# Loading phi a second time with tokens on partitions, in place of turning it on TensorE

## The chip, the cores and the metric

The kernel runs on one NeuronCore of a Trainium2 chip. The metric is the device time of one execution in microseconds (us). The kernel before took 540.55 us (median of three runs, 540.34 to 540.92). Five engines work side by side and meet only at semaphores: PE (TensorE: matmuls and transposes through an identity matrix), DVE (VectorE), ACT (ScalarE), POOL (GpSimd) and SP (SyncE, which here only issues DMAs). Each works off its own instructions strictly in order.

## The reference

For each of 8 batches and 8 heads, 576 tokens attend to 32 "memories"; the result goes through a bilinear feed-forward network.

```python
a = phi - np.max(phi, axis=2, keepdims=True)        # phi (b, h, s, m): the max is over the tokens s
a = np.exp(a)
a = a / (np.sum(a, axis=2, keepdims=True) + 1e-09)  # and so is the sum
k_m = np.einsum('bhsm,bhsd->bhmd', a, k)            # contraction over the tokens
v_m = np.einsum('bhsm,bhsd->bhmd', a, v)
scores = scale * np.matmul(q, k_m.transpose(0, 1, 3, 2))
attn = softmax(scores) over m;  attn_out = attn @ v_m
x = attn_out as (tokens, 512);  out = ((x @ w1) * (x @ w2)) @ w3 @ w_out
```

The two ways in which `phi` is used pull apart: maximum and sum run over the tokens, so they want the tokens along the free dimension; the contraction `a^T k` runs over the tokens as well, and a matmul contracts over the partitions, so it wants the tokens there.

## The kernel before, in words

Weights are converted and multiplied together once, at the start (a long order written out by hand, `START`). Then a loop runs over the 8 batches. In iteration b PE does for batch b the two large products: 16 units "A" (`ab_unit`, L528: 12 matmuls each, 6 into a PSUM bank `a` and 6 into a bank `b`), and then the output products "O" (`out_part`, L558). Between them it does the attention of batch b+1 and the first attention steps of batch b+2. The order of PE's and SP's instructions is the order of the lists `FIRST`, `SECOND` and `STEADY` (L44 to L54), word by word; a "+" after a word means batch b+2, and `phi3`, `kv3`, `q2` are the loads of batches b+3 and b+2. In the loop DVE's and ACT's orders are not written by hand: a scheduler chooses them.

One unit "A" works like this: PE fills `a` (6 matmuls) and `b` (6 matmuls); ACT copies `a` to SBUF (`a_sb`, L550); DVE multiplies `b` by `a_sb` to `gr` (L553); ACT rounds `gr` to `gh` (L130); DVE computes the rest `gl = gr - gh` (L132). The banks `a` and `b` exist twice each, so PE may write bank `b` of unit n+2 only when `gr` of unit n is done, and bank `a` of unit n+2 when `a_sb` of unit n is done.

The first attention steps of a batch, in iteration b for batch b+2: `phi` is loaded with (head, memory) on the 128 partitions and the 576 tokens along the free dimension, in two halves t of four heads each (tile `ph`, 128x1152, DMA at L143). Then

- `top` (L183): DVE takes the negated maxima, one per partition and half: `mx`, 128x2.
- `exp` (L189): two ACT instructions, exp(ph + mx) in place, and the sums `sm` on the way.
- `norm` (L198): two small DVE instructions turn `sm` into its reciprocal.
- `turn0`, `turn4` (L203): PE transposes 8 and 1 blocks of 128x128 of `ph` into PSUM, ACT copies them to the tile `a` (128x1024 at L213 and 128x128 at L218): now the tokens are on partitions.
- `mem` (L220): 80 small matmuls of `a` with `kv`, after the 16 units A; ACT scales the result by `sm`.

The tile `a` shares its place in SBUF with `s_sb`, the scores of the batch whose attention is being computed after `mem`.

SP issues all loads and stores. In an iteration of the steady kind the last store of the output products (L585) is issued just after PE has begun the next iteration's first unit A, since ACT must copy the result out of PSUM first (L584). The next DMAs in SP's order are the `kv` loads (L154), which wait until `mem` has freed the place of the previous `kv`.

The iterations that turn a batch of number 3 or more: iteration 1 turns batch 2 (as the word `turn0`) and batch 3 (as `turn0+`); iterations 2 to 5 turn batches 4 to 7.

Of the kernel before, what the change touches and what calls it, by code (L numbers as in the profile page):

```python
# [8 lines left out]
F32 = mybir.dt.float32  # L9
# [4 lines left out]
AF = mybir.ActivationFunctionType  # L14
ALU = mybir.AluOpType
# [29 lines left out]
O O blocks O sc0 sc1p Mp se0 q2 sn0 O O kv2 pr0 O O O se1 sn1 O Mp Mp M O pr1 O phi2 O O O O O  # L45
""".split()
SECOND = """
A top exp A norm turn0 A turn4 A phi2 mem A kv2 blocks A A A A top+ A exp+ A norm+ A turn0+ A A turn4+ A A
mem+ sc0 sc1p Mp O kv3 se0 O se1 O q2 sn0 O pr0 O sn1 O pr1 M Mp Mp O O phi3 O O blocks+ O O O O O O Oo Oo Oo Oo
""".split()  # L50
STEADY = """
A top+ A exp+ A norm+ A A turn0+ A A turn4+ A A A A A A A A A
mem+ sc0 sc1p Mp O kv3 se0 O se1 O q2 sn0 O pr0 O sn1 O pr1 M Mp Mp O O phi3 O O blocks+ O O O O O O Oo Oo Oo Oo
""".split()  # L54


# [1 line left out]
def memory_attention__then__bilinear_ffn_kernel(  # L58
# [2 lines left out]
    qT: bass.AP,  # L61
    kv: bass.AP,
    phiT: bass.AP,
    weights: bass.AP,
    out: bass.AP,
):
# [10 lines left out]
    nc = tc.nc  # L77
    P = 128
    B, NG, S = qT.shape[0], 4, 576
    D = 64  # L80
    M = 32
    NT = 2
    DF = 1024
    weights = weights.bitcast(I32)
# [5 lines left out]

    const = ctx.enter_context(tc.tile_pool(name="const", bufs=1))
    att = ctx.enter_context(tc.tile_pool(name="att", bufs=1))
    ps_ab = ctx.enter_context(tc.tile_pool(name="ps_ab", bufs=2, space=bass.MemoryType.PSUM))
    ps_o = ctx.enter_context(tc.tile_pool(name="ps_o", bufs=2, space=bass.MemoryType.PSUM))
    ps_x = ctx.enter_context(tc.tile_pool(name="ps_x", bufs=1, space=bass.MemoryType.PSUM))
# [15 lines left out]
    for x, where in (("h", Wh), ("l", Wl)):  # L111
        t = const.tile([P, half, DO], F32R, name=f"W{x}0")
# [21 lines left out]
    def whole(step):  # L134
        for _ in step:
            pass


    loaded = {}
# [25 lines left out]
        loaded["q", b] = t  # L165
        yield

    LOADS = {"phi": load_phi, "kv": load_kv, "q": load_q}

    def load(what, b):  # L170
        b += int(what[-1])
        if b < B:
            return LOADS[what[:-1]](b)
        return ()
# [4 lines left out]
    def attention(b):  # L179

        v = {}

        def top():  # L183
            v["ph"] = loaded.pop(("ph", b))
            v["mx"] = att.tile([P, NT], F32, name="mx")
            nc.vector.tensor_reduce(out=v["mx"], in_=v["ph"], axis=AX.X, op=ALU.max, negate=True)
            yield

        def exp():  # L189
            v["sm"] = att.tile([P, NT], F32, name="sm")  # L190
            ph, mx, sm = v["ph"], v["mx"], v["sm"]
            for t in range(NT):
                nc.scalar.activation(
                    out=ph[:, t], in_=ph[:, t], func=AF.Exp, bias=mx[:, t : t + 1], accum_out=sm[:, t : t + 1]
                )
                yield

        def norm():  # L198
            nc.vector.tensor_scalar_add(v["sm"], v["sm"], 1e-9)
            nc.vector.reciprocal(out=v["sm"], in_=v["sm"])  # L200
            yield

        def turn(i):  # L203
            ps = psum_pair().rearrange("p k (c t x) -> p (k c) t x", c=2, t=NT)
            if i == 0:
                for c in range(4):
                    for t in range(NT):
                        at = t * D + c * P
                        nc.tensor.transpose(ps[:, c, t], v["ph"][:, t, at : at + P], ident)  # L209
                yield  # L210
                a = att.tile([P, 5 * NT * P], F32, name="a", tag="a")
                v["a"] = a.rearrange("p (c t x) -> p c t x", t=NT, x=P)
                nc.scalar.copy(out=v["a"][:, :4], in_=ps)  # L213
            else:
                last = v["ph"].rearrange("p t s -> p (t s)")[:, 4 * P : 5 * P]
                nc.tensor.transpose(ps[:, 0, 0], last, ident)
                yield
                nc.scalar.copy(out=v["a"][:, 4, 0], in_=ps[:, 0, 0])  # L218
# [84 lines left out]
        def probs(n):  # L303
# [7 lines left out]
            yield  # L311
            yield from split(ah[:, n], al[:, n], v["at"][:, n])

        steps = {"top": top, "exp": exp, "norm": norm, "mem": memories, "blocks": blocks}
        steps |= {f"turn{i}": lambda i=i: turn(i) for i in (0, 4)}
        for n in range(2):
            steps |= {f"sc{n}": lambda n=n: scores(n, pair), f"sc{n}p": lambda n=n: scores(n, banks_ab)}
# [7 lines left out]
    def memory_weights(b):  # L325

        ms = ready["M", b] = []

        def step(q, banks):
            one = None if banks else psum_pair()  # L330
            ps = banks() if banks else [one[:, t] for t in range(NT)]
            for g in range(NG):
                for t in range(NT):
                    d = slice((1 - t) * D, (2 - t) * D)
                    nc.tensor.matmul(  # L335
                        ps[t][g * M : (g + 1) * M],
                        lhsT=vm[b % 2][d, g],
                        rhs=w12_sb[q][d, :, g],
                        start=True,
                        stop=True,  # L340
                    )
            yield
            mh = const.tile([P, NT, 2, FQ], F32R, name=f"mh{q}", tag=f"m{m_tags[2 * q]}")
            ml = const.tile([P, NT, 2, FQ], F32R, name=f"ml{q}", tag=f"m{m_tags[2 * q + 1]}")
            if banks:
                for t in range(NT):
                    yield from split(mh[:, t], ml[:, t], ps[t].rearrange("p (w f) -> p w f", w=2))
            else:
                yield from split(mh, ml, one.rearrange("p t (w f) -> p t w f", w=2))
            ms.append((mh, ml))  # L350
            yield

        return [lambda banks=None, q=q: step(q, banks) for q in range(NQ)]
# [125 lines left out]
    def by_hand():  # L479
        return tc.manual_schedule(engines=set(HAND) | {mybir.EngineType.Activation, mybir.EngineType.DVE})  # L480

    steps = [attention(b) for b in range(B)]
    m0 = memory_weights(0)
    a0 = [(n, 2 * q + f) for q in range(NQ) for n in range(2) for f in range(2)]
    under_way = {}

    def begin(what):
        name, digits = what.rstrip("0123456789."), what.lstrip("abcdefghijklmnopqrstuvwxyzACGHKLNW")
        if name in LOADS:
            return load(what, 0)  # L490
# [67 lines left out]
    def out_part(b, i, part, v):  # L558

        first = 0 if b % 2 else REST  # L560
        at = first + i * P
        if part == 0:
            v["p"] = psum(ps_o, "o")
        for f in range(part * NF // 4, (part + 1) * NF // 4):
            for k, (x, y) in enumerate(((gh, Wh), (gl, Wh), (gh, Wl))):
                nc.tensor.matmul(  # L566
                    v["p"],
                    lhsT=x[f][:, at : at + P],
                    rhs=y[f],
                    start=f == 0 and k == 0,  # L570
                    stop=f == NF - 1 and k == 2,
                )
        if part < 3:
            return
        osb = big.tile([P, DO], F32, name="osb", bufs=2)
        if at == 0:
            nc.scalar.copy(out=osb, in_=v["p"])
            for j in range(2):
                c = (b - 1 + j) * S
                nc.sync.dma_start(out=out[c : c + REST], in_=osb[j * REST : (j + 1) * REST])  # L580
            return
        c = b * S + at - b % 2 * REST
        if b + 1 < B or at + P < S:
            nc.scalar.copy(out=osb, in_=v["p"])  # L584
            nc.sync.dma_start(out=out[c : c + P], in_=osb)  # L585
        else:
            for j, copy in enumerate((nc.scalar.copy, nc.vector.tensor_copy)):
                x = slice(j * DO // 2, (j + 1) * DO // 2)
                copy(out=osb[:, x], in_=v["p"][:, x])
                nc.sync.dma_start(out=out[c : c + P, x], in_=osb[:, x])  # L590
# [5 lines left out]
    for b in range(B):  # L596
        v = {}
# [5 lines left out]
        def emit(what):  # L603
# [4 lines left out]
            elif what == "Oo":  # L608
                if b % 2:
                    out_part(b, *next(parts), v)  # L610
            elif what[:-1] in LOADS:
                whole(load(what, b))
# [11 lines left out]
            emit(what)  # L624


_INS = ["qT", "kv", "phiT", "weights"]
_OUT = (4608, 512)


# [52 lines left out]
```

## Time and profile before

| | |
|---|---|
| Time, median of three runs | 540.55 us (540.34 to 540.92) |
| The profiled execution: its time, its span | 540.96 us, 539.0 us |
| Busy: PE, DVE, ACT | 525.2 us (97%), 310.1 us (58%), 252.8 us (47%) |
| Granted TensorE clock | 1.0 (full) |
| DMA queues of the program | 30.8% of 16 engines' span |
| Instructions | 9799 |

The span runs from the first instruction to the last; 1.96 us of the execution lie around it. PE's matmuls overlap, so one matmul's duration is longer than the time by which it moves the next one on; the chain of work that ended last gives each group of PE's matmuls the time that it really took up.

### The profile page before, as it was taken

Reading aid. Unit: us, or ns where it says so; the run is one execution under the profiler, and the core shown is the slowest. Engines: PE = TensorE matmul, PEld = TensorE weight load, DVE = VectorE, ACT = ScalarE, POOL = GpSimd, SP = SyncE. Lnnn points to the kernel's source line nnn. Section 1 sums busy time; section 2 is a strip of 40 time slices with the busy share of each in tenths; the row PEclk is TensorE's granted clock in tenths of the full one; section 3 lists DMA queues with packets and bytes.
Section 4 is the critical chain, followed back from the end, with each engine's and each line's share of the span. In section 5 each row is a group of like instructions: output and inputs, shape, how many; then the busy total and the mean of one; then the engine's idle time right before and its main releaser. Section 6 shows DMA issues by size and latency. Waiting matters only on the chain.

```text
span 539.0 us, 9799 instructions
## 1 busy us (share of the span) xinstructions
PE 525.2 (97%) x4056; PEld 432.8 (80%) x4056; DVE 310.1 (58%) x594; ACT 252.8 (47%) x510; POOL 0.7 (0%) x6
## 2 busy tenths in 40 slices
PE   4999989999999999999999999999999999999997
PEld 1457678868996799868986899769986898689985
DVE  5889999493658425683569235763577056905400
ACT  6998886353654325443544244344544144414310
POOL 0000000000000000000000000000000000000000
PEclk9999999999999999999999999999999999999999
DMA  8999616082607210342015200631021100010011
GB/s 335 420 419 420 272 45 264 2 294 93 221 1 283 84 39 2 123 183 82 1 63 223 102 20 1 223 125 40 2 89 40 39 21 2 21 58 2 1 39 60
DMA packets 14940, 64.07 MB, mean 119 GB/s; under 512 B 1712, under 2 KB 1968, under 8 KB 10032
## 3 DMA queue, kind: packets, MB, share of 16 engines
q1 hardware_dynamic: 14896, 63.45, 30.8%
q8 instruction: 32, 0.52, 0.4%
q14 instruction: 12, 0.10, 0.1%
HBM read 54.00 MB, written 9.44 MB: 118 GB/s over the span
## 4 chain that ended last, share of the span: by engine, by line
PE 92%; DVE 5%; DMA 1%; ACT 1%; issue 1%; DVEq 0%; ACTq 0%
PE o L566 37%; PE a L540 18%; PE b L540 18%; PE a L463 3%; PE b L463 3%; PE a L335 2%; PE o L228 2%; PE x L335 2%; DVE w L417 1%; PE x L209 1%; PE b L335 1%; PE x L228 1%; DMA ph<-in_phiT 1%; PE o L463 1%; PE x L270 1%
## 5 line engine op out<-in xcount | busy, mean ns | idle before, releaser
L553 DVE TENSOR_TENSOR gr<-b,a_sb 128x288 f32<-128x288 f32 x128 | 58.2, 457 | 85.4 <-PE b L540 83.1
L130 ACT CAST gh<-gr 128x288 fp32r<-128x288 f32 x128 | 55.3, 435 | 97.6 <-DVE gr L553 97.4
L566 PE MATMUL o<-W,gh 128*128 128x512 f32 x288 | 96.7, 396 | 0.0
L132 DVE TENSOR_TENSOR gl<-gr,gh 128x288 fp32r<-128x288 f32 x128 | 58.4, 458 | 57.2 <-ACT gh L130 56.9
L540 PE MATMUL b<-ah,mh 128*128 128x288 f32 x256 | 75.5, 295 | 1.7 <-DVE gr L553 1.7
L540 PE MATMUL a<-ah,mh 128*128 128x288 f32 x256 | 77.0, 301 | 0.1
L540 PE MATMUL b<-al,mh 128*128 128x288 f32 x256 | 75.5, 295 | 0.0
L540 PE MATMUL a<-ah,ml 128*128 128x288 f32 x256 | 75.5, 295 | 0.0
L540 PE MATMUL a<-al,mh 128*128 128x288 f32 x256 | 75.5, 295 | 0.0
L540 PE MATMUL b<-ah,ml 128*128 128x288 f32 x256 | 75.4, 294 | 0.0
L566 PEld LDWEIGHTS o<-W,gh 128*128 128x128 f32 x288 | 54.1, 188 | 17.3 <-issue 5.9
L584 ACT COPY osb<-o 128x512 f32<-128x512 f32 x31 | 18.1, 585 | 100.3 <-PE o L566 88.2
L566 PE MATMUL o<-Wh,gh 128*128 128x512 f32 x144 | 57.1, 397 | 0.0
L566 PE MATMUL o<-Wh,gl 128*128 128x512 f32 x144 | 56.4, 392 | 0.0
L566 PE MATMUL o<-Wl,gh 128*128 128x512 f32 x144 | 56.4, 392 | 0.0
L566 PE MATMUL o<-W,gl 128*128 128x512 f32 x144 | 56.4, 391 | 0.0
L550 ACT COPY a_sb<-a 128x288 f32<-128x288 f32 x128 | 50.4, 396 | 3.7 <-PE a L540 3.4
L540 PEld LDWEIGHTS a<-ah,mh 128*128 128x128 f32 x256 | 48.1, 188 | 3.3 <-issue 1.0
L540 PEld LDWEIGHTS b<-ah,mh 128*128 128x128 f32 x256 | 48.1, 188 | 2.4 <-DVE gr L553 2.2
L540 PEld LDWEIGHTS a<-al,mh 128*128 128x128 f32 x256 | 48.2, 188 | 0.3
L540 PEld LDWEIGHTS b<-ah,ml 128*128 128x128 f32 x256 | 48.1, 188 | 0.0
L540 PEld LDWEIGHTS a<-ah,ml 128*128 128x128 f32 x256 | 48.1, 188 | 0.0
(134 smaller groups left out, 770.3 us busy)
## 6 DMA issues: line engine op xcount, KB each, us to landing
kv<-in_kv SPq DMA_DIRECT2D x16, 1024.0 KB, 7.1
raw<-in_weights SPq DMA_DIRECT2D x10, 1024.0 KB, 18.0
q<-in_qT SPq DMA_DIRECT2D x8, 1152.0 KB, 10.0
out<-osb SPq DMA_DIRECT2D x31, 256.0 KB, 2.0
raw<-in_weights SPq DMA_DIRECT2D x12, 512.0 KB, 9.1
ph<-in_phiT SPq DMA_DIRECT2D x8, 576.0 KB, 4.1
kv<-in_weights SPq DMA_DIRECT2D x3, 1024.0 KB, 16.6
kv<-in_kv SPq DMA_DIRECT2D x8, 256.0 KB, 8.4
```

What stands on the lines that cost most here:

```text
L130: nc.scalar.copy(out=hi, in_=src)
L132: nc.vector.tensor_tensor(out=lo, in0=src, in1=hi.bitcast(F32), op=ALU.subtract)
L209: nc.tensor.transpose(ps[:, c, t], v["ph"][:, t, at : at + P], ident)
L228: nc.tensor.matmul(ps[t][h * M : (h + 1) * M, : 2 * D], lhsT=v["a"][:, i, t, h * M : (h + 1) * M], rhs=kvt[i][:, (4 * t + h) * 2 * D : (4 ...
L270: nc.tensor.matmul(ps[t][g * M : (g + 1) * M], lhsT=km[b % 2][t * D : (t + 1) * D, g], rhs=v["q"][t * D : (t + 1) * D, g, n * HALF : (n + ...
L335: nc.tensor.matmul(ps[t][g * M : (g + 1) * M], lhsT=vm[b % 2][d, g], rhs=w12_sb[q][d, :, g], start=True, stop=True,)
L463: nc.tensor.matmul(pw[r][i], lhsT=x[:, i * P : (i + 1) * P], rhs=y, start=k == 0 and j == 0, stop=k == NF - 1 and j == len(pairs) - 1,)
L540: nc.tensor.matmul(p, lhsT=x[:, t, w, fc : fc + P], rhs=y[:, n, t * HALF : (t + 1) * HALF], start=i == 0, stop=i == len(todo) - 1,)
L550: nc.scalar.copy(out=a_sb, in_=ps[0])
L553: nc.vector.tensor_tensor(out=gr, in0=ps[1], in1=a_sb, op=ALU.mult)
L566: nc.tensor.matmul(v["p"], lhsT=x[f][:, at : at + P], rhs=y[f], start=f == 0 and k == 0, stop=f == NF - 1 and k == 2,)
L584: nc.scalar.copy(out=osb, in_=v["p"])
```

## The change

From batch 3 on PE no longer turns `phi`. Instead `phi` is loaded a second time (`load_rows`), laid out by the host with the tokens on partitions, straight into the tile `a`. There the maxima are needed as a row along the free dimension, the same on all partitions. So:

- `row`: DVE's 32x32 block transpose turns the 128x2 maxima, padded to 128x32 (`mx32`, which POOL once sets to zero), into `turned`; four DMAs of 2x32 elements write them to a small tensor in HBM; one DMA reads it back as a row of 256 elements for each of the 128 partitions (`all`).
- `less`: one DVE instruction of 128x1024 and two of 64x128 add the (negated) maxima to `a`; one ACT instruction takes exp of 128x1152 in place.

`top`, `exp` and `norm` stay as they were: the sums `sm` still come from the first copy. The word `row+` stands in the lists behind `top+`, `less+` before the last five units A, `rows3` (the second load, of batch b+3) behind `phi3`. Batches 0 to 2 are turned on PE as before.

```diff
 SECOND = """
-A top exp A norm turn0 A turn4 A phi2 mem A kv2 blocks A A A A top+ A exp+ A norm+ A turn0+ A A turn4+ A A
-mem+ sc0 sc1p Mp O kv3 se0 O se1 O q2 sn0 O pr0 O sn1 O pr1 M Mp Mp O O phi3 O O blocks+ O O O O O O Oo Oo Oo Oo
+A top exp A norm turn0 A turn4 A phi2 mem rows2 A kv2 blocks A A A A top+ row+ A exp+ A norm+ A A A less+ A A
+mem+ sc0 sc1p Mp O kv3 se0 O se1 O q2 sn0 O pr0 O sn1 O pr1 M Mp Mp O O phi3 rows3 O O blocks+ O O O O O O Oo Oo Oo Oo
 """.split()
 STEADY = """
-A top+ A exp+ A norm+ A A turn0+ A A turn4+ A A A A A A A A A
-mem+ sc0 sc1p Mp O kv3 se0 O se1 O q2 sn0 O pr0 O sn1 O pr1 M Mp Mp O O phi3 O O blocks+ O O O O O O Oo Oo Oo Oo
+A top+ row+ A exp+ A norm+ A A A A A A A A less+ A A A A A
+mem+ sc0 sc1p Mp O kv3 se0 O se1 O q2 sn0 O pr0 O sn1 O pr1 M Mp Mp O O phi3 rows3 O O blocks+ O O O O O O Oo Oo Oo Oo
 """.split()
...
+    def load_rows(b):
+        t = att.tile([P, 5 * NT * P], F32, name="a", tag="a")
+        loaded["rows", b] = t
+        nc.sync.dma_start(out=t[:, : 9 * P], in_=phi[b])
+        yield
...
         def top():
             v["ph"] = loaded.pop(("ph", b))
-            v["mx"] = att.tile([P, NT], F32, name="mx")
+            v["mx"] = mx32[:, :NT] if b >= BY_ROWS else att.tile([P, NT], F32, name="mx")
             nc.vector.tensor_reduce(out=v["mx"], in_=v["ph"], axis=AX.X, op=ALU.max, negate=True)
...
+        def row():
+            turned = att.tile([P, M], F32, name="turned")
+            nc.vector.transpose(out=turned, in_=mx32)
+            mx = dram.tile([NT, NG, M], F32, name="mx")
+            for g in range(NG):
+                nc.sync.dma_start(out=mx[:, g], in_=turned[g * M : g * M + NT])
+            v["all"] = att.tile([P, NT * P], F32, name="all")
+            nc.sync.dma_start(out=v["all"], in_=mx.rearrange("t g m -> (t g m)").partition_broadcast(P))
+            yield
+
+        def less():
+            a = loaded.pop(("rows", b))
+            v["a"] = a.rearrange("p (c t x) -> p c t x", t=NT, x=P)
+            x = a[:, : 8 * P].rearrange("p (c x) -> p c x", c=4)
+            mx = v["all"].rearrange("p (c x) -> p c x", c=1)
+            nc.vector.tensor_tensor(out=x, in0=x, in1=mx.broadcast_to([P, 4, NT * P]), op=ALU.add)
+            for t in range(NT):
+                x = a[t * D : (t + 1) * D, 8 * P : 9 * P]
+                nc.vector.tensor_tensor(out=x, in0=x, in1=v["all"][t * D : (t + 1) * D, t * P : (t + 1) * P], op=ALU.add)
+            yield
+            a = a[:, : 9 * P]
+            nc.scalar.activation(out=a, in_=a, func=AF.Exp)
+            yield
...
+    BY_ROWS = 3
+    mx32 = const.tile([P, M], F32, name="mx32")
+    nc.gpsimd.memset(mx32, 0.0)
     steps = [attention(b) for b in range(B)]
```

Where the words of `less` land in DVE's and ACT's orders is the scheduler's choice. In the program `less+` stands behind the eleventh unit A of a steady iteration. DVE's order in iteration 3 around the first units A (each `gr` and each `gl` is one unit's) was before:

```order
L186 TENSOR_REDUCE mx<-ph 128x2
L199 TENSOR_SCALAR sm<-sm 128x2
L200 RECIPROCAL sm<-sm 128x2
L553 TENSOR_TENSOR gr<-b,a_sb 128x288
L132 TENSOR_TENSOR gl_624<-gr,gh_616 128x288
L553 TENSOR_TENSOR gr<-b,a_sb 128x288
L132 TENSOR_TENSOR gl_624<-gr,gh_616 128x288
L553 TENSOR_TENSOR gr<-b,a_sb 128x288
L132 TENSOR_TENSOR gl_625<-gr,gh_617 128x288
L553 TENSOR_TENSOR gr<-b,a_sb 128x288
```

and the same place now:

```order
L194 TENSOR_REDUCE mx_92<-ph 128x2
L208 STREAM_TRANSPOSE turned<-mx_92 128x32
L231 TENSOR_SCALAR sm<-sm 128x2
L232 RECIPROCAL sm<-sm 128x2
L588 TENSOR_TENSOR gr<-b,a_sb 128x288
L134 TENSOR_TENSOR gl_628<-gr,gh_620 128x288
L588 TENSOR_TENSOR gr<-b,a_sb 128x288
L134 TENSOR_TENSOR gl_628<-gr,gh_620 128x288
L588 TENSOR_TENSOR gr<-b,a_sb 128x288
L221 TENSOR_TENSOR a<-a,all 128x1024
L224 TENSOR_TENSOR a<-a,all 64x128 x2
L134 TENSOR_TENSOR gl_629<-gr,gh_621 128x288
```

The three instructions of `less` (L221, L224) stand behind the third unit's `gr`, ahead of its `gl` and of the fourth unit's `gr`; iterations 2, 4 and 5 have the same order. For batch 3, in iteration 1, they stand behind the eleventh unit's `gr`.

ACT's order in iteration 3, from the third unit's copy on (`gh` are the casts of `gr`), is now:

```order
L585 COPY a_sb<-a 128x288
L132 CAST gh_621<-gr 128x288
L585 COPY a_sb<-a 128x288 x2
L227 ACTIVATE a<-a 128x1152
L132 CAST gh_621<-gr 128x288
L132 CAST gh_622<-gr 128x288
L585 COPY a_sb<-a 128x288 x2
```

The new exp (L227) stands behind the fifth unit's copy and ahead of the fourth unit's cast; the copies of PSUM to `a` (L213, L218) are gone from it.

SP's order at the border of iterations 2 and 3, from the load of `phi` in iteration 2 to the `kv` loads of iteration 3, was before:

```order
L143 DMA ph<-in_phiT 128x1152
L585 DMA out<-osb 128x512 x2
L154 DMA kv_3113<-in_kv 128x2048
L154 DMA kv_3115<-in_kv 128x2048
L159 DMA kv_3117<-in_kv 128x512
```

and is now:

```order
L145 DMA ph<-in_phiT 128x1152
L173 DMA a<-in_phi 128x1152
L620 DMA out<-osb 128x512 x2
L211 DMA mx<-turned 2x32 x4
L213 DMA all<-mx 128x256
L156 DMA kv_3117<-in_kv 128x2048
```

The four small writes and the read stand behind the last store of an iteration; the read waits for all four writes, the writes for DVE's transpose.

More of the change, by code (lines that the diff above doesn't have):

```diff
@@ L63, in memory_attention__then__bilinear_ffn_kernel @@
     phiT: bass.AP,
+    phi: bass.AP,
     weights: bass.AP,
@@ L92, in memory_attention__then__bilinear_ffn_kernel @@
     att = ctx.enter_context(tc.tile_pool(name="att", bufs=1))
+    dram = ctx.enter_context(tc.tile_pool(name="dram", bufs=2, space=bass.MemoryType.DRAM))
     ps_ab = ctx.enter_context(tc.tile_pool(name="ps_ab", bufs=2, space=bass.MemoryType.PSUM))
@@ L166, in load_q @@
         yield
-    LOADS = {"phi": load_phi, "kv": load_kv, "q": load_q}
+    def load_rows(b):
[3 more added lines that the diff above has]
+        yield
+    LOADS = {"rows": load_rows, "phi": load_phi, "kv": load_kv, "q": load_q}
     def load(what, b):
@@ L312, in probs @@
             yield from split(ah[:, n], al[:, n], v["at"][:, n])
-        steps = {"top": top, "exp": exp, "norm": norm, "mem": memories, "blocks": blocks}
+        steps = {"top": top, "row": row, "less": less, "exp": exp, "norm": norm, "mem": memories, "blocks": blocks}
         steps |= {f"turn{i}": lambda i=i: turn(i) for i in (0, 4)}
@@ L624, in memory_attention__then__bilinear_ffn_kernel @@
             emit(what)
-_INS = ["qT", "kv", "phiT", "weights"]
+_INS = ["qT", "kv", "phiT", "phi", "weights"]
 _OUT = (4608, 512)
@@ L663 @@
         tiles.append(x.ravel())
+    rows = phi.reshape(b, h // 2, 2, s, m).transpose(0, 3, 2, 1, 4).reshape(b, s, 2, h // 2 * m)
+    rows = np.concatenate(
+        [
+            rows[:, :whole].reshape(b, whole // p, p, -1).transpose(0, 2, 1, 3).reshape(b, p, -1),
+            rows[:, whole:].transpose(0, 2, 1, 3).reshape(b, p, -1),
+        ],
+        axis=-1,
+    )
     laid = {
+        "phi": rows,
         "qT": q.transpose(0, 1, 3, 2).reshape(b, h // 2, 2 * d, s).transpose(0, 2, 1, 3).reshape(b, 2 * d, -1),
```

## The prediction

> **What bounds the kernel now.** I read the page first, its busy times and its chain of work that ended last:
>
> ```profile
> PE 525.2 (97%) x4056; PEld 432.8 (80%) x4056; DVE 310.1 (58%) x594; ACT 252.8 (47%) x510; POOL 0.7 (0%) x6
> ...
> PE 92%; DVE 5%; DMA 1%; ACT 1%; issue 1%; DVEq 0%; ACTq 0%
> ```
>
> PE works nearly without a break, and 92% of the chain is PE. So an instruction taken from PE shortens the run by what it takes up there, as long as nothing new makes PE wait. Next comes the chain in the phase of iteration 3 in which batch 5 is turned. Its columns are start, length, what:
>
> ```profile
> 251.47 0.79 PE a L540 x6
> ...
> 259.40 0.87 PE x L209 x8
> ...
> 263.44 0.11 PE x L216
> ...
> 277.05 0.79 PE b L540 x6
> ```
>
> The 16 units A run from 251.47 to 277.05 + 0.79 = 277.84, 26.37 us, and the two pieces of turning stand in the chain with 0.87 and 0.11. The same phase of iteration 6, where nothing is turned:
>
> ```profile
> 429.95 0.79 PE a L540 x6
> ...
> 455.34 0.65 PE x L270 x16
> ```
>
> It takes 455.34 - 429.95 = 25.39 us, so a unit takes 25.39/16 = 1.587, and the difference, 26.37 - 25.39 = 0.98, is just 0.87 + 0.11. PE does not wait for the turning today; it only pays for it.
>
> **What is removed.** Five such pairs (batches 3 to 7): 5 x 0.98 = 4.9 us off PE. That ACT no longer copies the blocks out of PSUM is worth nothing by itself, since ACT is at 47%.
>
> **What is added, off the path.** DVE's 128x32 transpose stands between the maxima and the reciprocal of the sums. DVE's timeline there:
>
> ```profile
> 248.19 0.17 DVE L199 TENSOR_SCALAR sm<-sm 128x2 f32<-128x2 f32 x1 [1.82 <-ACT ph L193]
> 248.40 0.17 DVE L200 RECIPROCAL sm<-sm 128x2 f32<-128x2 f32 x1
> ...
> 256.33 0.46 DVE L553 TENSOR_TENSOR gr<-b,a_sb 128x288 f32<-128x288 f32 x1 [0.17 <-PE b L540]
> ```
>
> DVE sits idle for 1.82 us right after the maxima, so the transpose (nearest rows 0.17 and 0.46) is free. If that cover were gone, the next `gr` is still 4 us away. The second load of `phi` is issued behind the first, so it delays no load that DVE waits for. The waiting of SP for the four writes holds back the `kv` loads behind it in the queue, but these wait for the memory matmuls at 277.84 anyway.
>
> **What is added on a tight path.** The first `gr` to the fourth `gr` decide. DVE now does `less` directly behind the third unit's `gr`, which ends at 256.33 + 0.46 = 256.79. Its price, from the grouped rows:
>
> ```profile
> L258 DVE TENSOR_SCALAR km<-x 64x128 f32<-64x128 f32 x16 | 4.5, 284 | 16.9 <-PE x L254 16.9
> ...
> L447 DVE TENSOR_TENSOR m<-w,m 128x1024 fp32r<-128x1024 f32 x3 | 3.7, 1218 | 0.1
> ```
>
> One instruction like L447 (1.22) and two like L258 (0.29 each): 1.80 us. Behind them stand the third `gl` and the fourth `gr`, 0.46 each. PE needs the fourth `gr` before it may write bank `b` of the sixth unit. The first unit's `b` starts in PE's timeline at
>
> ```profile
> 252.09 0.29 PE L540 MATMUL b<-ah,mh 128*128 128x288 f32 x1
> ```
>
> so the sixth unit's, with no turning between, at 252.09 + 5 x 1.587 = 260.03. Counted back: minus 0.05 for the hand-over (0.04 lie between DVE's two rows at 248), minus 2 x 0.46, minus 1.80: `less` must start by **257.26**, 0.47 after DVE is free for it. Were its data there, PE would not notice.
>
> ACT's share: the exp comes behind `less` and ahead of two casts and the sixth unit's copy. ACT's timeline has the sizes:
>
> ```profile
> 260.00 0.43 ACT L130 CAST gh<-gr 128x288 fp32r<-128x288 f32 x1 [0.85 <-DVE gr L553]
> 260.33 1.01 ACT L213 COPY a<-x 128x1024 f32<-128x1024 f32 x1
> 261.24 0.40 ACT L550 COPY a_sb<-a 128x288 f32<-128x288 f32 x1
> ```
>
> 1152 elements at L213's pace are 1.13 us. With `less` from 257.26 to 259.06 the exp ends at 260.2, two casts and the copy at 261.5. Bank `a` of the eighth unit, which needs that copy, is due 7 units after the first unit's `a`, 251.47 + 7 x 1.587 = 262.6. About 1 us to spare, so ACT's part costs nothing.
>
> But `less` needs `all`, and that is a round trip through HBM which cannot begin before SP has issued the iteration's last store:
>
> ```profile
> 246.66 5.83 SPq L585 DMA_DIRECT2D out<-osb  x2
> ```
>
> SP is free at 246.66 + 5.83 = 252.49; the writes' data have long been ready by then. No row shows a DMA of 2x32 or one that reads back what was just written. The nearest, by issue time and landing (minimum, median, maximum), from the views of the lines L590 (128 KB each, rows of 1 KB), L580 (128 KB, 64 partitions) and L143 (loads of `phi`, 576 KB):
>
> ```profile
> L590 SPq DMA_DIRECT2D out<-osb x2: 332/341/350, 535.8 to 536.3; - x2
> ...
> DMA to landing us min/median/max: 1.7/1.7/1.7
> ```
>
> ```profile
> L580 SPq DMA_DIRECT2D out<-osb x8: 472/566/590, 171.1 to 514.5; - x8
> ...
> DMA to landing us min/median/max: 2.2/2.9/3.8
> ```
>
> ```profile
> DMA to landing us min/median/max: 3.6/4.1/8.6
> ```
>
> and from the page, stores of rows of 2 KB:
>
> ```profile
> out<-osb SPq DMA_DIRECT2D x31, 256.0 KB, 2.0
> ```
>
> - *Issue*: 0.34 (L590) to 0.59 (L580). I take 0.34, since L590's transfers have the smallest rows. The fourth write is issued at 252.49 + 3 x 0.34 = 253.51.
> - *Write landing*: halving 256 KB to 128 KB saved 0.3, so 1.4 is the lower end; 2.9 (L580) the upper. I take 1.85, between the rows of 1 KB and of 2 KB, because these rows are shorter still and must be placed one by one. Landed at 255.36; `all` is issued at 255.41.
> - *Read landing*: 128 KB. The lower end is 1.7, of a store of that size. Upper: L143's fastest, 3.6, less 0.3 for each of the 3.5 times 128 KB that it moves more, 2.55. I take the middle, 2.1. `all` is there at 257.51, `less` starts at 257.56.
>
> That is 257.56 - 257.26 = **0.30 us too late**, and PE stands still for as long at the sixth unit's bank `b`, in each of the iterations 2 to 5. DVE then catches up, since behind the stall it has the same slack as before.
>
> Sum: -4.9 + 4 x 0.30 = -3.7. Against the profiled execution's own 540.96: 537.3. The median of the runs shown, 540.55, is 0.41 below that execution: **536.9 us**.
>
> The ends: with 1.4 and 1.7, `less` could start at 252.49 + 1.02 + 1.4 + 0.05 + 1.7 + 0.05 = 256.71, and nothing is lost: 535.65. With 0.59, 2.9 and 2.55 it is 259.81, 2.55 late, four times 10.2: 545.9. No gain below zero hides in these: an earlier row cannot make PE faster than its own instructions.
>
> [...]
>
> **Batch 3** has its own place. In iteration 1 `less` stands behind the eleventh `gr`, and SP issues the writes behind three `kv` loads and the second `phi` load. The chain and SP's timeline:
>
> ```profile
> 150.97 0.79 PE b L540 x6
> ```
>
> ```profile
> 139.47 0.81 SPq L154 DMA_DIRECT2D kv<-in_kv  x2
> 140.78 0.33 SPq L159 DMA_DIRECT2D kv<-in_kv  x1
> ```
>
> The piece is the eleventh unit's `b`, so its `gr` (0.46) ends at about 151.76 + 0.5 = 152.3, 11 us after SP is free for the writes at 141.1. Even if these land only behind all four loads (22.5 times 128 KB, at 0.3 each 6.8 us from 139.5 on, and 1.85 more: 148.2), `all` is there by 150.3 and in time; I count this batch with its full 0.98.
>
> **The rivals.**
>
> *The round trip is hidden whole.* For it: 0.3 us decides, and the payload of the writes is 1 KB. Against it: the read is 128 KB. The time is 540.55 - 4.9 = 535.65. [...]
>
> *The round trip eats the gain, and more.* Place: DVE behind the third `gr`, in iterations 2 to 5. Price: 4 us for each us that `all` is late. It decides from 4.9/4 = 1.23 late, that is `all` landing after 258.44, and then the change is slower; at the upper end it is 545.9. For it: L580's landing of 2.9 and issue of 0.57 are those of the smallest number of partitions in the trace, and the writes have two each. Against it: L590. [...]
>
> *Something in between*, 0.9 to 1.5 late: between 539.25 and 541.65, about what it was.
>
> *It does not do what it says:* the subtraction was to come late in A, but DVE's order has it behind the third unit. Were it executed behind the eleventh, this would be the first rival.
>
> **How the numbers follow.** Forecast, late by up to 0.9: 0.50. Hidden whole: 0.25. In between: 0.12. Eaten up: 0.13. A difference of 0.2% (1.1 us) is about what a measurement of this kernel can tell from none; it is left where the delay is 0.95 to 1.5. So faster 0.75, same 0.12, slower 0.13. The range starts a little under the first rival, 535.4, and ends at 540.2, where the delay is 1.14, which leaves out most of the last case and a part of the one before.
>
> **What would show it.** PE's transposes (64 and 8 of 128x128) fall to 24 and 3. `less` waits for the DMA of `all` in iterations 2 to 5, by DVE's waits, and PE's `b` of the sixth unit waits for `gr` by about 0.3 each. A phase A of iteration 3 takes 25.4 plus that wait. It would be wrong if PE waited elsewhere (behind the exp, for `a_sb`, or for `mem`), if the writes took turns rather than running at once, or if phase A stayed at 26.4.

## The result, and the profile after

The changed kernel took 538.25 us (median of seven runs) beside 540.59 for the kernel before on the same chip: ratio 0.995, interval 0.9933 to 0.9967. Repeated later with five runs and a profile of its own it took 537.38 beside 540.15: ratio 0.9947, interval 0.9935 to 0.996. So it is faster by 2.3 to 2.8 us. (The first profiled execution of the changed kernel ran at a mean granted clock of 0.56, and is left aside; all rows below are from the repeated one, at a mean clock of 0.999.)

The page of the changed kernel, its span and its busy times:

```profile
span 536.3 us, 9765 instructions
...
PE 521.4 (97%) x4011; PEld 428.2 (80%) x4011; DVE 317.7 (59%) x614; ACT 251.6 (47%) x505; POOL 0.8 (0%) x7
```

PE has 45 instructions less, DVE 20 more, and the span is 539.0 - 536.3 = 2.7 us shorter, not 4.9. The grouped rows (L221 and L224 are `less`; L241 and L248 are the transposes that are left, of batches 0 to 2):

```profile
L221 DVE TENSOR_TENSOR a<-a,all 128x1024 f32<-128x1024 f32 x5 | 6.1, 1226 | 4.8 <-DMA all<-mx 4.8
...
L241 PE MATMUL x<-ident,ph 128*128 128x128 f32 x24 | 3.2, 275 | 0.2 <-DVE ml L134 0.2
...
L224 DVE TENSOR_TENSOR a<-a,all 64x128 f32<-64x128 f32 x10 | 2.8, 283 | 0.1
...
L248 PE MATMUL x<-ident,ph 128*128 128x128 f32 x3 | 0.8, 272 | 0.0
```

The transposes fell as they should, and `less` costs 1.23 + 2 x 0.28. But DVE stands idle for 4.8 us in all ahead of it, waiting for the row `all`. What that does to PE stands in the table of waits (us in total, times, longest):

```profile
DVE a L221 <- DMA all<-mx: 4.8, 5, 1.0
...
PE b L575 <- DVE gr L588: 2.5, 7, 1.4
```

Before, PE waited twice for `gr`, 1.7 us in all; now five more times. The chain through the beginning of iteration 3 (start, length, what) shows each step of the round trip, and that PE hangs on it:

```profile
250.56 0.60 ACT osb L619
...
251.17 0.34 SPq L620
251.51 0.05 issue
251.56 0.02 SPq L211
...
251.60 0.26 SPq L211
...
252.22 0.24 SPq L211
252.46 0.04 issue
252.51 1.22 DMA mx<-turned
...
253.87 2.86 DMA all<-mx
256.73 0.02 issue
256.75 0.13 DVE a L221
...
257.89 0.28 DVE a L224
...
258.18 0.29 DVE a L224
258.47 0.03 issue
258.50 0.46 DVE gl L134
258.96 0.38 DVE gr L588
259.34 0.04 issue
259.38 1.06 PE b L575 x6
```

Read from the top: the last store of iteration 2 is issued (SPq L620), then the four writes of the maxima, 0.30 us apart. The chain has three of their issues; its piece `DMA mx` begins with the issue of the fourth, at 252.51, and ends with its landing at 253.73. So does the piece of the read, which takes 2.86; `less` runs from 256.75 to 258.47, the third `gl` and the fourth `gr` follow, and only then may PE write bank `b` of the sixth unit. PE's timeline has the first and the last matmul of this phase, and the pause:

```profile
250.31 0.29 PE L575 MATMUL a<-ah,mh 128*128 128x288 f32 x1
...
259.38 0.40 PE L575 MATMUL b<-ah,mh 128*128 128x288 f32 x1 [0.19 <-DVE gr L588]
...
276.02 0.29 PE L575 MATMUL b<-ah,ml 128*128 128x288 f32 x1
```

The idle time shown, 0.19, is less than what is lost: `b` should follow 0.13 behind the last matmul of `a` at 258.90, at 259.03, and the matmul after it follows 0.24 behind instead of 0.13. That is 0.35 + 0.11 = 0.46.

**One measure for all kernels below.** I take the time from the start of the first to the start of the last matmul of a phase A, as in these rows: 276.02 - 250.31 = 25.71. In iterations 6 and 7, which turn nothing and read no row, it is 25.25 to 25.26 in every kernel. What an iteration has over 25.25 is what the turning or the round trip costs it. Iteration 1 also turns batch 2 and does its small matmuls; its own undisturbed length is 28.94, which is 29.93 of the kernel before less the 0.99 of one turning (the last kernel but one below reaches 28.95).

| us over the undisturbed length | iteration 1 (batch 3) | 2 | 3 | 4 | 5 | sum | first unit of iteration 1 starts at | span |
|---|---|---|---|---|---|---|---|---|
| before | 0.99 | 0.99 | 0.98 | 0.99 | 0.99 | 4.95 | 130.46 | 539.0 |
| changed (`again`) | 0.44 | 0.46 | 0.46 | 0.46 | 0.45 | 2.27 | 130.54 | 536.3 |
| `late` | 0.59 | 3.00 | 3.00 | 3.00 | 3.01 | 12.6 | 129.37 | 545.4 |
| `no_trip` | 0.63 | 0 | 0 | 0 | 0 | 0.63 | 130.97 | 535.0 |
| `early` | 0.66 | 0 | 0.78 | 0 | 0 | 1.44 | 129.78 | 534.7 |
| `two_writes` | 0.28 | 0.35 | 0.33 | 0.43 | 1.26 | 2.65 | 132.27 | 538.4 |
| `late3` | 0.55 | 0 | 0 | 0 | 0.01 | 0.56 | 130.88 | 535.0 |
| `early2` | 5.36 | 0 | 0.89 | 0 | 0.02 | 6.27 | 130.00 | 539.7 |
| `twice` | 2.20 | 2.00 | 1.74 | 2.19 | 1.88 | 10.0 | 129.34 | 542.9 |
| `best3` | 0.01 | 0 | 0 | 0 | 0 | 0.01 | 129.49 | 533.1 |

Span, sum and start belong together (the start part is all that stands ahead of the first unit of iteration 1, iteration 0 included): the span of the kernel before, plus the difference of the sums, plus the difference of the starts, gives each span to 0.2 us. For the changed kernel it is 539.0 - (4.95 - 2.27) + 0.08 = 536.4, measured 536.3. For `best3`, 539.0 - 4.94 - 0.97 = 533.1. So the phases A account for the whole effect, and what is left between two profiles is when the start part ended, which differs by up to 3 us between these profiles; the two spans of `two_writes` that lie furthest apart, 535.7 and 538.4, show that executions of one kernel differ by nearly as much.

### The profile page after: what moved, and what is told of

It reads as the page before. It is cut to its first block, busy times and chain, and to the rows that moved or that the text cites. A ratio compares the mean times of both kernels' runs of the same rounds, so it can differ in the third digit from the quotient of the medians.

```text
span 866.4 us, 9765 instructions
## 1 busy us (share of the span) xinstructions
PE 855.5 (99%) x4011; PEld 570.4 (66%) x4011; DVE 320.6 (37%) x614; ACT 261.3 (30%) x505; POOL 0.8 (0%) x7
## 4 chain that ended last, share of the span: by engine, by line
PE 99%; DMA 0%; ACT 0%; DVE 0%; SPq 0%; issue 0%; ACTq 0%
PE o L601 38%; PE b L575 19%; PE a L575 19%; PE a L495 4%; PE b L495 4%; PE a L367 2%; PE o L495 2%; PE x L367 2%; PE o L260 2%; PE b L367 1%; PE x L260 1%; PE x L302 1%; PE a L302 1%; PE x L241 1%; DMA raw<-in_weights 0%; PE x L286 0%
## 5 line engine op out<-in xcount | busy, mean ns | idle before, releaser
L601 PE MATMUL o<-W,gh 128*128 128x512 f32 x288 | 145.3, 576 | 0.0
L575 PE MATMUL a<-ah,mh 128*128 128x288 f32 x256 | 105.7, 413 | 0.0
L575 PE MATMUL b<-ah,ml 128*128 128x288 f32 x256 | 105.0, 410 | 0.0
L575 PE MATMUL b<-al,mh 128*128 128x288 f32 x256 | 104.9, 410 | 0.0
L575 PE MATMUL b<-ah,mh 128*128 128x288 f32 x256 | 104.8, 409 | 0.0
L575 PE MATMUL a<-al,mh 128*128 128x288 f32 x256 | 104.6, 409 | 0.0
L575 PE MATMUL a<-ah,ml 128*128 128x288 f32 x256 | 104.0, 406 | 0.0
L601 PE MATMUL o<-W,gl 128*128 128x512 f32 x144 | 83.5, 580 | 0.0
L601 PE MATMUL o<-Wl,gh 128*128 128x512 f32 x144 | 83.3, 578 | 0.0
L601 PE MATMUL o<-Wh,gh 128*128 128x512 f32 x144 | 82.9, 576 | 0.0
L601 PE MATMUL o<-Wh,gl 128*128 128x512 f32 x144 | 82.9, 576 | 0.0
L575 PEld LDWEIGHTS b<-al,mh 128*128 128x128 f32 x256 | 56.2, 219 | 4.3
```

Source lines behind the costliest of these rows:

```text
L575: nc.tensor.matmul(p, lhsT=x[:, t, w, fc : fc + P], rhs=y[:, n, t * HALF : (t + 1) * HALF], start=i == 0, stop=i == len(todo) - 1,)
L601: nc.tensor.matmul(v["p"], lhsT=x[f][:, at : at + P], rhs=y[f], start=f == 0 and k == 0, stop=f == NF - 1 and k == 2,)
```

## The experiments

Four theories. *Round trip*: 4.9 us were gained, and each iteration gives some back because `less` waits for the row. *Insertion*: it is the 1.8 us of `less` on DVE and the 1.2 us of exp on ACT, put between the units, that hold PE up, whether the row is there or not. *Small gain*: taking the transposes off PE was worth less than 4.9 from the start. *Batch 3*: the part missing beyond iterations 2 to 5 is lost in iteration 1. The kernels are told in the order in which the argument needs them.

### The changed kernel once more

No edit.

> The changed kernel once more, for a profile at full clock and a second timing. Three theories of why 4.9 us were taken off PE and only some 2.5 came out. Round trip: the addition of the maxima on DVE waits for the row of maxima from HBM, in iterations 2 to 5; PE then stands still 0.5 to 0.7 us before bank b of the sixth unit A, four times; time 538. Insertion: the addition finds its data, and the 1.8 us of DVE and 1.2 us of ACT in the middle of A make PE wait, at the sixth unit or later; time 538. Gross gain: PE does not wait in phase A at all, but the phase takes more than 25.4 us without the turning; time 538.

Ratio 0.9947 (0.9935 to 0.996). The round trip's theory has its chain and its 0.46 in each of the iterations 2 to 5. Batch 3, which I had counted as free, loses 0.44 as well; the chain in iteration 1:

```profile
143.30 0.25 SPq L211
143.56 0.04 issue
143.60 6.69 DMA mx<-turned
...
150.43 2.90 DMA all<-mx
...
153.35 0.14 DVE a L221
```

The last of the writes takes 6.69 us from its issue, against 1.22 in iteration 3: three `kv` loads and the second `phi` load are issued ahead of it.

### The round trip left out

```diff
-            mx = dram.tile([NT, NG, M], F32, name="mx")
-            for g in range(NG):
-                nc.sync.dma_start(out=mx[:, g], in_=turned[g * M : g * M + NT])
-            v["all"] = att.tile([P, NT * P], F32, name="all")
-            nc.sync.dma_start(out=v["all"], in_=mx.rearrange("t g m -> (t g m)").partition_broadcast(P))
+            v["all"] = zeros
...
+    zeros = const.tile([P, NT * P], F32, name="zeros")
+    nc.gpsimd.memset(zeros, 0.0)
```

> Leaves out the round trip through HBM: the addition adds a row of zeros that was set once, so the maxima are not subtracted in the second copy of phi; the four writes and the read per batch are gone. The scheduler then puts the addition ahead of the first unit A, where DVE is idle. Round trip and insertion: both costs are gone, 535.7. Gross gain: 538, since PE's work is the same as in the changed kernel.

536.12, ratio 0.992 (0.9908 to 0.9932); this kernel leaves out the subtraction of the maxima. Iterations 2 to 5 lose nothing: turning on PE was worth all of its 0.99 there, and the theory of a small gain falls. With the row always at hand the scheduler put `less` ahead of the first unit, so this run does not say what `less` costs in the middle of A. In iteration 1 `less` moved ahead too and now waited for the second `phi` load itself; DVE stood idle for 0.26 us, and PE lost 0.63 behind it:

```profile
140.89 3.77 DMA a<-in_phi
```

### `less` in program order: two attempts

`late` emits the words of phase A of iterations 2 to 5 with DVE and ACT in the order of the program, not the scheduler's:

```diff
-        for what in (FIRST, SECOND, STEADY)[min(b, 2)]:
+        words = (FIRST, SECOND, STEADY)[min(b, 2)]
+        cut = words.index("mem+") if 2 <= b < B - 2 else 0
+        with tc.manual_schedule(engines=set(HAND) | {mybir.EngineType.Activation, mybir.EngineType.DVE}):
+            for what in words[:cut]:
+                emit(what)
+        for what in words[cut:]:
             emit(what)
```

> DVE and ACT do phase A of iterations 2 to 5 in the order of the program text, so the addition and the exp stand behind the eleventh unit A, 12 us later; everything else stays. Round trip: the row has long landed, nothing waits, 535.7 (the whole 4.9 gained). Insertion: the same 1.8 and 1.2 us stand in the middle of A as before, 538. Gross gain: 538.

A miss: 548.12, ratio 1.0142 (1.0128 to 1.0156). Two of its waits:

```profile
PE a L575 <- ACT a_sb L585: 9.9, 8, 1.5
...
DVE a L221 <- DMA all<-mx: 1.1, 1, 1.1
```

The wait for the row is gone from iterations 2 to 5 (the one left is batch 3's), so the edit did that; but program order moved more than `less`. The maxima, the exp and `norm` came between the first units, and the exp of `less` directly behind it in ACT's queue. There a copy `a_sb` that PE needed stood behind an exp that was itself waiting for DVE: in the chain of iteration 3 the last addition of `less` ends at 273.82, the exp starts at 273.85, and the copy only at 274.92. Two pauses per iteration, eight in all, are what the row of PE shows. The second pause of an iteration, 1.52 us, is that of the exp of `less`. The 3.0 us per iteration are the price of where these stood, not of the amount of work, as the second attempt shows. `late3` keeps the scheduler's order up to the unit behind `norm` and splits the exp off as a word of its own, three units later:

```diff
-A top+ row+ A exp+ A norm+ A A A A A A A A less+ A A A A A
+A top+ row+ A exp+ A norm+ A A A A A A A A less+ A A A lexp+ A A
...
+            v["rows"] = a[:, : 9 * P]
             yield
-            a = a[:, : 9 * P]
-            nc.scalar.activation(out=a, in_=a, func=AF.Exp)
+
+        def lexp():
+            nc.scalar.activation(out=v["rows"], in_=v["rows"], func=AF.Exp)
             yield
...
+        n, cut = (words.index("norm+") + 2, words.index("mem+")) if 2 <= b < B - 2 else (0, 0)
+        for what in words[:n]:
+            emit(what)
+        with tc.manual_schedule(engines=set(HAND) | {mybir.EngineType.Activation, mybir.EngineType.DVE}):
+            for what in words[n:cut]:
+                emit(what)
```

> In iterations 2 to 5 DVE and ACT follow the program text from the third unit A on, and the text puts the addition behind the eleventh unit and the exp behind the fourteenth, so that ACT does not stand waiting for the addition; maxima, exp of the first copy and reciprocal are left to the scheduler as in the changed kernel. Round trip: the row has landed 10 us before, no wait in these iterations, 535.5. Insertion: 1.8 us on DVE and 1.2 us on ACT in the middle of A cost what they cost before, 537.4.

536.4, ratio 0.9916 (0.9904 to 0.9929): 4.5 us faster than before. DVE's timeline in iteration 3:

```profile
269.38 1.22 DVE L221 TENSOR_TENSOR a<-a,all 128x1024 f32<-128x1024 f32 x1
270.51 0.58 DVE L224 TENSOR_TENSOR a<-a,all 64x128 f32<-64x128 f32 x2
```

Nothing stands in brackets: DVE does not wait here. The same 1.8 us on DVE and the same exp on ACT stand between the units, and iterations 2 to 5 lose nothing. For this place the theory of insertion falls. For the place in the changed kernel, behind the third `gr`, the next run decides.

### The round trip doubled

```diff
-            nc.sync.dma_start(out=v["all"], in_=mx.rearrange("t g m -> (t g m)").partition_broadcast(P))
+            for _ in range(2):
+                nc.sync.dma_start(out=v["all"], in_=mx.rearrange("t g m -> (t g m)").partition_broadcast(P))
```

> The row is read from HBM twice, one read after the other, into the same tile, so it is there 3.0 us later; DVE's order has the addition one unit A later, behind the fourth gr (twelfth for batch 3). Round trip: each of the five waits grows from 0.45 by 3.0 less one unit's 1.59, to 1.9, in sum 7 us more, 544.5. Insertion: 537.4.

545.18, ratio 1.0087 (1.0074 to 1.01), slower than before. The scheduler moved `less` one unit later, so that not all of the 2.9 us of the second read reaches PE; the losses grow from 0.46 to 1.7 to 2.2 us per iteration. Its waits:

```profile
DVE a L222 <- DMA all<-mx: 12.5, 5, 2.7
...
PE b L576 <- DVE gr L589: 10.2, 7, 1.9
```

and DVE's timeline in iteration 3:

```profile
261.72 1.23 DVE L222 TENSOR_TENSOR a<-a,all 128x1024 f32<-128x1024 f32 x1 [2.24 <-DMA all<-mx]
```

DVE's wait of 2.24 us and PE's loss of 1.74 in the table differ by 0.50. In the changed kernel it is 0.95 and 0.46, and so it goes in the iterations 2 to 5 of the changed kernel, of `twice` and of `two_writes` (below): twelve waits of 0.82 to 2.69 us, each with a loss that is 0.49 to 0.50 shorter. In this range every further us of waiting cost PE one, and followed back from these twelve the line reaches, as my estimate, no loss at a wait of 0.5 us, with the 1.8 us of `less` in place. By this estimate insertion falls for the changed kernel too: what costs is the wait for the row, as far as it is longer than 0.5 us. No run had the row there in time at this very place. This run is the side of the balance on which the change loses.

### The row sooner

`two_writes` writes the maxima with two DMAs of 4x32 in place of four of 2x32:

```diff
-            for g in range(NG):
-                nc.sync.dma_start(out=mx[:, g], in_=turned[g * M : g * M + NT])
+            for i in range(NT):
+                nc.sync.dma_start(out=mx[i], in_=turned[i::M])
```

> The maxima go to HBM in two DMAs of 4x32 in place of four of 2x32; DVE's and ACT's orders do not change. Round trip: two issues of 0.3 us fall away from the way to the row, more than the 0.46 us for which PE stands still in each of the iterations 2 to 5, so these four waits go and 535.5 is left; batch 3, whose writes wait behind the kv loads, keeps its 0.44. Insertion: the additions and the exp are where they were, so 537.4.

A miss in two ways. The view of line L211:

```profile
L211 SPq DMA_DIRECT2D mx<-turned x10: 483/508/642, 144.3 to 369.5; - x10
```

One issue now takes 0.51 us where one of half the rows took 0.25 (median of the changed kernel): SP spends about as long on two as on four. The way from SP's turning to the writes to the row took 5.04 us in iteration 3 instead of 5.17 (251.56 to 256.73 in the chain above), and iterations 2 to 4 lose 0.33 to 0.43 instead of 0.46; in iteration 5 the second write took 2.48 from its issue to its landing, where it took 1.51 in iteration 3, DVE waited 1.76 for the row, and it cost 1.26. By the phases, then, nothing is gained (2.65 against 2.27). The total, 539.06 (ratio 0.9964, 0.995 to 0.9977), cannot be compared, because of something in the start part, which the edit does not touch. DVE's timeline there:

```profile
76.78 1.35 DVE L194 TENSOR_REDUCE mx<-ph 128x2 f32<-128x1152 f32 x1 [3.04 <-DMA ph<-in_phiT]
```

and PE's:

```profile
78.92 0.41 PE L575 MATMUL b<-ah,mh 128*128 128x288 f32 x1 [3.55 <-DVE gr L588]
```

It is the same mechanism in another place: maxima that wait for a load stand ahead of `gr` in DVE's queue. In the changed kernel the same wait was 0.92 and PE's pause 1.42. Why the load came later here is not shown.

`early` does `top` and `row` of batches 4 to 7 one part earlier, in the last third of the iteration before, among the output products:

```diff
-A top+ row+ A exp+ A norm+ A A A A A A A A less+ A A A A A
+A A exp+ A norm+ A A A A A A A A less+ A A A A A
...
-...phi3 rows3 O O blocks+ O O O O O O Oo Oo Oo Oo
+...phi3 rows3 O O blocks+ O O top3 row3 O O O O Oo Oo Oo Oo
...
+            elif what in ("top3", "row3"):
+                if b + 3 < B:
+                    whole(steps[b + 3][what[:-1]]())
```

> For batches 4 to 7 the maxima, DVE's transpose, the four writes and the read are written one store earlier in SP's order (behind the third store of the iteration before, rather than behind its last), some 5.5 us sooner; the addition then stands ahead of the first unit A in DVE's order. Round trip: the row lands at about the start of the first unit A, 535.7 to 536.2. Insertion: 535.7 to 536.2 as well, since the addition has left the middle of A. Gross gain: 538.

537.09, ratio 0.9936 (0.9923 to 0.995); the interval overlaps the changed kernel's, so by time alone the two are not told apart, and the 535.7 to 536.2 expected were missed. By phases they are told apart: iterations 2, 4 and 5 lose nothing, iteration 3 loses 0.78. The scheduler had now put `less` ahead of the first unit's `gr`, and in iteration 3, whose first unit starts at 249.30, the row was still not early enough for that place:

```profile
251.14 1.23 DVE L221 TENSOR_TENSOR a<-a,all 128x1024 f32<-128x1024 f32 x1 [4.35 <-DMA all<-mx]
```

The last write took 2.1 us from its issue to its landing here, where it took 1.2 in the iterations 2, 4 and 5. In iterations 2 and 4 the row came over 4 us ahead of the first unit; in iteration 5 it came 1.0 us behind the unit's start, just early enough. Moving the row forward does not help where the scheduler moves its reader forward by as much.

`early2` adds to this an order for batch 3 in which the writes go out ahead of the `kv` loads, to win the 0.4 us of iteration 1:

```diff
-... mem rows2 A kv2 blocks A A A A top+ row+ A exp+ A norm+ A A A less+ A A
+... mem rows2 A blocks A A A A top+ row+ kv2 A exp+ A norm+ A A A less+ A A
```

> The kernel with the round trip one store earlier, and in iteration 1 the kv loads of batch 3 behind the writes and the read of its row, so that these no longer queue behind 2.3 MB. Round trip: the 0.44 us of batch 3 goes as well, and the whole 4.9 is gained, 535.2. If the kv loads, now later, are missed by the memory matmuls of batch 3, that shows as a new wait there.

A miss: 541.93, ratio 1.0022 (1.0005 to 1.0039). The writes now landed in 1.28 us, but the scheduler drew `less` ahead, from behind the eleventh `gr` to behind the sixth, the read took 4.54 beside the `kv` loads, and PE stood still:

```profile
150.90 0.41 PE L575 MATMUL b<-ah,mh 128*128 128x288 f32 x1 [3.52 <-DVE gr L588]
```

This pause does not yet make the 5.36 of the table. The rest shows in PE's clock, the third number from the end, in stretches of 1 us:

```profile
152.00:153.00 1.00, 1.00 (x7) 1.00 (x6) 0.87 (x3) 0.50 (x2) 0.00 (x0) 0.59 0.76 303
153.00:154.00 1.00, 1.00 (x6) 1.00 (x6) 0.32 (x1) 0.73 (x2) 0.00 (x0) 0.50 0.18 70
154.00:155.00 1.00, 1.00 (x6) 1.00 (x5) 0.35 (x1) 0.00 (x0) 0.00 (x0) 0.50 0.02 8
155.00:156.00 1.00, 1.00 (x8) 1.00 (x7) 0.86 (x3) 0.47 (x2) 0.00 (x0) 0.70 0.00 0
```

From about 152.2 to 155.6 PE works at half the clock, beginning 1.3 us after the pause, and loses another 3.4/2 = 1.7 us.

### A version that beats both

`best3` is `late3` with batch 3 set right by hand as well: writes ahead of the `kv` loads, then DVE and ACT in program order, `less` two units behind `norm`.

```diff
-... mem rows2 A kv2 blocks A A A A top+ row+ A exp+ A norm+ A A A less+ lexp+ A A
+... mem rows2 A blocks A A A A top+ row+ kv2 exp+ norm+ A A less+ A A A lexp+ A A
...
-        n, cut = (words.index("norm+") + 2, words.index("mem+")) if 2 <= b < B - 2 else (0, 0)
+        n, cut = (words.index("norm+") + 1 + (b > 1), words.index("mem+")) if 1 <= b < B - 2 else (0, 0)
```

> The kernel with the addition behind the eleventh unit and the exp behind the fourteenth, now for batch 3 as well (iteration 1), and there with the kv loads behind the writes and the read of the row, so that these no longer queue behind 2.3 MB, while the addition cannot move ahead of the eleventh unit. Round trip: none of the five waits is left, the whole 4.9 us is gained, ratio 0.991, 0.4 us below the kernel in which batch 3 still waited. If the memory matmuls of batch 3 wait for the later kv loads, that shows at their place.

535.24, ratio 0.9902 (0.989 to 0.9915): by the ratio 5.3 us faster than before, and faster than the changed kernel, whose interval begins at 0.9933. One row of its waits is enough:

```profile
PE b L577 <- DVE gr L590: 2.0, 2, 1.9
```

Two waits as before the change (both in the start part), none for the row, and iteration 1 is back at 28.95. All of the 4.9 us is there. The profile's 5.9 holds another 0.97 from an earlier end of the start part.

`best4` goes one batch further and loads batch 2 by rows too (`BY_ROWS = 2`):

```diff
-... pr1 O phi2 O O O O O
+... pr1 O phi2 rows2 O top+ row+ O O O O
...
-A top exp A norm turn0 A turn4 A phi2 mem rows2 A ...
+A exp A norm A less lexp A phi2 mem rows2 A ...
```

> As the last one, and batch 2 by rows too: its second load of phi, its maxima and its round trip stand in iteration 0, its additions ahead of the first unit A of iteration 1. A sixth pair of transposes (0.98 us) leaves PE: 1.0 us below the last one, ratio 0.989, if the row of batch 2 lands before the first unit A; if it does not, PE waits there for a gr, and the gain is smaller by that wait.

A miss: 539.77, ratio 0.999 (0.9973 to 1.0006), no change against before. The maxima of batch 2 wait for its `phi` until 126.7, and by the chain the writes then stand in SP's order behind a store, whose result ACT copies only behind the exp of `phi`, until 130.7. So the row is not there when `less` stands at the head of DVE's queue (a wait of 6.0 us). PE's timeline and the stretch behind it:

```profile
138.44 0.40 PE L577 MATMUL b<-ah,mh 128*128 128x288 f32 x1 [2.81 <-DVE gr L590]
```

```profile
141.00:142.00 1.00, 1.00 (x6) 1.00 (x5) 1.00 (x3) 0.34 (x2) 0.00 (x0) 0.50 0.00 0
```

A further 0.98 gained cost 5.0 us: 32.96 us for the phase, where 28.94 - 0.98 = 27.96 were due. A second stretch at half clock lies in this profile's start part, from 78.1 to 81.6. Whether a later `less` could win that 0.98 was not tried.

## Why the prediction was right, and where it was not

Predicted 536.9, range 535.4 to 540.2; measured 538.25 and 537.38. The mechanism forecast as the likeliest is the one that the chain shows. Step by step:

- **Gain of 0.98 per turning.** Right: 0.99 by the phases, and `late3` and `best3` get it back whole.
- **DVE's transpose and ACT's exp cost nothing.** Right for the changed kernel. The transpose took 0.21 us at 245.77, long before the row was needed, and the table of waits has none of PE for `a_sb`. The exp is free by its place, though: in `late`, where it stood ahead of a copy that PE needed, it cost 1.5 us per iteration.
- **`less` must start by 257.26 (in the old times), 0.47 behind DVE's third `gr`.** Right in place. The phase starts 1.00 earlier in the new trace (250.31 against 251.31), so the due time is 256.26; `less` started at 256.75, 0.49 late, and PE lost 0.46. `less` with 1.72 us (256.75 to 258.47) for 1.80 was right within 0.1.
- **The row is 0.30 late.** The mechanism was right and the size off: it is 0.46. Two terms of the sum were mis-sized by more than the result, in opposite directions; that the sum came so near is luck:
  - the issues, from SP's being free to the start of the fourth: taken 1.02, measured 1.00 (251.51 to 252.51);
  - landing of the writes, from the start of the last issue: taken 1.85, on the assumption that short rows land later, for which no run shows a price; measured 1.22, so 0.63 too long;
  - hand-over from the landing to the issue of the read: taken 0.05, measured 0.14;
  - landing of the read, from its issue, in the view of line L213: taken 2.1 between bounds of 1.7 and 2.55, measured 2.86 in this iteration and 2.85 to 2.90 in all five, so 0.76 too short. The upper bound was wrong. I got it from loads of full width, less their bytes; but this transfer reads one row of 1 KB for 128 partitions, and takes 1.2 longer than the 1.7 of a store of the same 128 KB. Whether the one row is the reason was not tried.

```profile
DMA to landing us min/median/max: 2.9/2.9/2.9
```

- **Batch 3 counts with its full 0.98.** Wrong, by 0.44. The step that failed is "`all` is there by 150.3": it landed at 153.3. With that, 2 us to spare became 1 us too late. SP came to the writes at 142.58 for 141.1, since the second `phi` load is issued ahead of the `kv` loads, but that was not what counted. I had the four loads end at 146.3 and the writes land 1.85 behind them. By the packets in the trace the loads' data moved until 150.7: 0.3 us for each 128 KB, taken from two stores, was too little for them. The writes' eight pieces of 128 B moved at 148.85 to 148.94, over 5 us behind the last issue, and landed at 150.29; in iteration 3 the pieces of the last write moved 0.7 us behind its issue, by 253.25, and landed at 253.73. The read then took 2.9. `best3` puts the writes ahead of the `kv` loads and loses nothing.
- **The rivals.** *Hidden whole*: not in the changed kernel, but the row a little earlier or `less` later gives it (`late3`). *Eaten up*: not reached, but `twice` shows the point to be near: with a round trip 2.9 us longer, and `less` one unit later, the kernel is slower than before. *Does not do what it says*: half true. In the program `less` stands behind the eleventh unit, in DVE's order behind the third, and `late3`, which restores that place (and moves the exp three units further), is 1.8 us better for it.

The sum with the measured terms is -4.95 + 4 x 0.46 + 0.44 = -2.7; the span shows -2.7.

## What to carry to other kernels

When work leaves the bounding engine for a path through memory, price the way there and back from when its queue is free, not from when the data are ready, and compare with the due time of the first instruction that shares an in-order queue with the waiting one. Then look where the scheduler has put the waiting instruction: late in the program is not late in the queue, and here that place alone took 1.8 of the 4.9 us. A repair that moves the source earlier may be undone by the scheduler (`early`); one that fixes the place of the reader was not (`late3`), provided that it leaves the order of the rest as it was, which `late` did not.

## What the runs showed of the hardware that was not expected

- **A pause costs more than itself, and not by its length alone.** Pauses of PE of 3.5 us (`early2`, and in the start part `two_writes`) and of 2.8 us (`best4`) were each followed, 0.8 to 1.3 us after work began again, by a stretch at half the clock (0.50 in the rows of `early2` and `best4` above), in which the 128x288 matmuls of one bank started 0.24 us apart, where it is 0.13 otherwise: from 152.2 to 155.6 in `early2`, from 79.7 to 82.9 at least in `two_writes`, from 139.8 to 142.8 at least in `best4`. So was, at once, one of 1.87 us in the start part of `best4` (78.1 to 81.6), but not one of 2.12 at the same place in `late3`. PE's timeline and a stretch behind it (the clock is again the third number from the end), first of `best4`, then of `late3`:

```profile
78.13 0.61 PE L577 MATMUL b<-ah,mh 128*128 128x288 f32 x1 [1.87 <-DVE gr L590]
```

```profile
79.00:80.00 1.00, 1.00 (x6) 1.00 (x6) 1.00 (x4) 1.00 (x5) 0.00 (x0) 0.50 0.00 0
```

```profile
78.19 0.40 PE L577 MATMUL b<-ah,mh 128*128 128x288 f32 x1 [2.12 <-DVE gr L590]
```

```profile
79.00:80.00 1.00, 1.00 (x9) 1.00 (x9) 1.00 (x4) 1.00 (x4) 0.00 (x0) 1.00 0.00 0
```

The longer of these two pauses is the one without the slow stretch, so the length alone does not decide; what does was not shown.
- **Half as many DMAs of twice the rows saved SP almost nothing.** Issuing one with two rows took 0.25 us, one with four rows 0.51. The number of rows is not the rule, for the read into 128 partitions took 0.34; what is was not tried.
- **The read of one row for all partitions** took 2.9 us, all five times in the changed kernel, and 2.85 to 3.0 in the other kernels; with the `kv` loads beside it, in `early2`, 4.54. In the changed kernel a 2x32 write took 1.2 us from its issue to its landing behind a single store (iteration 3), and 6.7 behind four loads (iteration 1).
- **The start part ended between 129.3 and 132.3 us** in kernels that hardly differ there. One part of this is shown, the wait of DVE's maxima for a load, and in `two_writes` the half clock behind it; the rest stays open. A difference of one profile's span below 3 us is read from the phases, not from the span.
